# The operands of the second layer's first token block: formed during the first layer's last slots, four of them in a pool of their own

## The chip, the cores and the metric

The kernel runs on one core of one Trainium2 chip. The metric is the device time of one execution in microseconds (us), the median over several runs. TensorE (PE) does the matmuls and PEld is its weight load; VectorE is DVE, ScalarE is ACT, GpSimd is POOL, and SyncE (SP) issues every DMA.

## What is computed

A Nyström attention over 4 batches, 8 heads, 576 positions and 64 dimensions gives 2304 tokens of 512 values. Two feed-forward layers follow:

```python
a = x @ w_a; b = x @ w_b            # 512 -> 1536
x = (a * b) @ w_out                 # 1536 -> 512     the first layer
h = x @ w_in                        # 512 -> 2048     the second layer
sp = np.where(h > 20.0, h, np.log1p(np.exp(np.minimum(h, 20.0))))
out = (h * np.tanh(sp)) @ w_out2    # 2048 -> 512
```

## The kernel before, in words

**Number format.** Every operand of the large matmuls is stored as two float32r parts, a rounded "hi" and a remainder "lo". `split` (L327) makes them: ACT copies the source into hi, then another engine (DVE here, POOL for the products of the first layer) subtracts hi from the source into lo. One product takes three matmuls per 128 rows: hi·hi, hi·lo, lo·hi.

**First layer.** It runs as 96 slots (the loop at L621). Each slot makes one 128-row piece of a and of b (`emit_ab`, 12 matmuls), multiplies them on DVE (tile tg), splits the result (tile g1; hi on ACT, lo on POOL) and takes one entry off the queue `o1q` (`emit_o1`, 12 matmuls that multiply four older g1 tiles by the output weights, added up in `x2acc`). After the last slot four entries are left, and L661 to L663 emit them; all four read the g1 tiles of slots 92 to 95. Finished x2acc tiles are stored to DRAM (x2d) by L468. Beside slots 57 to 88 the weights of the second layer are converted and stored (`u2`, `to_dram`).

**Second layer.** It takes the tokens in three blocks of 768 (index pr) and the 2048 columns in eight chunks, which makes 24 steps n (the loop at L790). A block is four quadrants of x, "11", "12", "21", "22", each 384 tokens by 256 values. The product with a chunk of `w_in` is Winograd's form of Strassen's scheme, seven products instead of eight (`ORDER = 1, 6, 2, 7, 5, 4, 3`). The x operand of product k is a quadrant or a signed sum: t1 = 12 − 11, t2 = 22 − t1, t3 = 22 − 12, t4 = 21 − t2 (`X_OF`, L712). A product is 6 matmuls of 384 columns into one of two `ab` banks. What it gives is combined by DVE on eviction (u2s, c11, u3s, c22, u4s, c21, c12), passed through Mish on ACT and split again (g2). The weight operands are sums too (`weight_sums`, L499): `convert(n)` makes those of chunk n in the first block (four DVE sums, three splits) and stores them for the later blocks; `convert_o(n)` does the same for the output weights. After each product, the loop emits one or two of the twelve groups (`emit_o2`, 3 matmuls of 512 columns each) that multiply the previous step's g2 by the output weights; the list `GROUPS` gives their order.

**What is made early.** `x_early` (L541) is called in slots 90 to 95. It loads the four quadrants of block 0 into `stg` buffers, forms t1 and t2 in place, splits the operands of products 1, 6 and 2 into the pool `wp`, and makes the weight sums of chunk 0. After the last slot, `load_quads(0)` (L778) loads the same four quadrants a second time, and L781 to L789 form t3, t1, t2, t4 and split operands 7, 5, 4, 3 into the pool `p2`.

**Memory.** The pools share SBUF by place: `main` (weights, bm, wab, attention factors, x2acc) and above it `p1` (ta, tg and nine g1 buffers) stand on the left; `wp` stands on the right. After the last `emit_o1`, `p1` and `main` are closed and `p2` takes their place from the left. Its tiles lie in the order in which the code first asks for them: the quadrants, the sums, the operands 7, 5, 4, 3, then m1, u2s, the two wc, s4, c11, m, g2, u3s, wo and the rest. `reuse_waits="tile"` means that a tile waits only for those older tiles whose bytes it covers.

**Order of the work.** From L592 on, no engine's order is written out: a planner simulates the program and puts every engine's instructions in the order in which they become ready there, the earlier line of the program first where several are ready. On the chip each engine, and SP's DMA queue too, then goes through its own list strictly in order.

Of the kernel before, what the change touches and what calls it, by code (L numbers as in the profile page):

```python
# [8 lines left out]
F32 = mybir.dt.float32  # L9
F32R = mybir.dt.float32r  # L10
AF = mybir.ActivationFunctionType
ALU = mybir.AluOpType
# [19 lines left out]
def nystrom_moe_kernel(ctx: ExitStack, tc: tile.TileContext, q, k, v, w_a, w_b, w_out1, w_in2, w_out2, out):  # L32
    nc = tc.nc
    NT = B * S
    ve, gp = nc.vector, nc.gpsimd
# [25 lines left out]
    main = main_ctx.enter_context(tc.tile_pool(name="main", bufs=1, side="left"))  # L61
# [265 lines left out]
    def split(dst_hi, dst_lo, src, hi_eng, lo_eng, pin=False):  # L327
        if hi_eng is ac:
            i = ac.activation(dst_hi, src, AF.Copy)
            if pin:  # L330
                tc.keep_in_program_order(i)
        else:
            hi_eng.tensor_copy(out=dst_hi, in_=src)
        lo_eng.tensor_tensor(dst_lo, src, dst_hi.bitcast(F32), op=ALU.subtract)  # L334
# [20 lines left out]
    wab = {}  # L355
# [91 lines left out]
    def emit_o1(b, gp_, hf, d, part):  # L447

        if part == 0:
            o1p[0] = bank("o1")  # L450
        p = o1p[0]
        g = 2 * gp_ + part
        for ch in range(2):
            w, x = wo1[2 * g + ch], g1[b, g, hf, ch]
            for n, (sl, sr) in enumerate(((0, 0), (0, 1), (1, 0))):
                first, last = (part, ch, n) == (0, 0, 0), (part, ch, n) == (1, 1, 2)
                pe.matmul(p[:, 0:288], w[:, sl, 128 * d:128 * d + 128], x[:, sr, :], start=first, stop=last)
        if part == 0:
            return
        if gp_ == 0 and d == 0:  # L460
            x2acc[b, hf] = main.tile([128, 4, 288], F32, tag="x2", bufs=4, name="x2acc")
        dst = x2acc[b, hf][:, d]
        if gp_ == 0:
            ac.activation(dst, p[:, 0:288], AF.Copy)
        else:
            ve.tensor_tensor(dst, p[:, 0:288], dst, op=ALU.add)
        if gp_ == 2 and d == 3:
            nc.sync.dma_start(out=x2d[b][:, :, 288 * hf:288 * hf + 288], in_=x2acc[b, hf])  # L468
# [24 lines left out]
    TB = 384  # L493
# [5 lines left out]
    def weight_sums(dst, src, t):  # L499
        a11, a12, a21, a22 = src[:, 0:2, 0:128], src[:, 2:4, 0:128], src[:, 0:2, 128:256], src[:, 2:4, 128:256]  # L500
        ve.tensor_tensor(t[:, 0], a21, a22, op=ALU.add)
        ve.tensor_tensor(t[:, 1], t[:, 0], a11, op=ALU.subtract)
        ve.tensor_tensor(t[:, 2], a11, a21, op=ALU.subtract)
        ve.tensor_tensor(t[:, 3], a12, t[:, 1], op=ALU.subtract)
        split(dst[:, 0, 0:2], dst[:, 1, 0:2], src[:, :, 0:128].rearrange("p (a j) f -> p a j f", a=2), ac, ve)
        split(dst[:, 0, 2], dst[:, 1, 2], a22, ac, ve)
        split(dst[:, 0, 3:7], dst[:, 1, 3:7], t, ac, ve)

    def load_quad(t, i, half):

        off = 0
        while off < TB:
            b, s0 = divmod(i * TB + off, S)
            n = min(TB - off, S - s0)
            nc.sync.dma_start(out=t[:, :, off:off + n], in_=x2d[b][:, 2 * half:2 * half + 2, s0:s0 + n])
            off += n
# [1 line left out]
    xs = {}  # L518

    def x_tile(pr, k):  # L520
        pool, tag, bufs = (wp, "xe", 3) if k in (1, 6, 2) else (p2, "xc", 5)
        t = xs[pr, k] = pool.tile([128, 2, 2, TB], F32R, tag=tag, bufs=bufs, name="xc")
        return t

    def split_x(pr, k, src):
        t = x_tile(pr, k)
        split(t[:, 0], t[:, 1], src, ac, ve)
# [3 lines left out]
    def wc_tile(k):  # L531
        pool, tag, bufs = (wp, "we", 1) if k % 3 == 0 else (p2, "wc", 2)
        t = wc[k] = pool.tile([128, 2, 7, 2, 128], F32R, tag=tag, bufs=bufs, name="wc")
        return t

    def stg(shape, nm):
        return base.tile(shape, F32, tag="stg", bufs=3, name=nm)

    early = {}

    def x_early(n):  # L541

        if n == 0:
            for q, (i, half) in (("11", (0, 0)), ("12", (1, 0)), ("22", (1, 1))):
                early[q] = stg([128, 2, TB], "x" + q)
                load_quad(early[q], i, half)
        elif n == 1:
            split_x(0, 1, early["11"])
        elif n == 2:
            ve.tensor_tensor(early["12"], early["12"], early["11"], op=ALU.subtract)  # L550
            ve.tensor_tensor(early["22"], early["22"], early["12"], op=ALU.subtract)
            early["21"] = stg([128, 2, TB], "x21")
            load_quad(early["21"], 0, 1)
        elif n == 3:
            split_x(0, 6, early["22"])
            early["w"] = stg([128, 4, 256], "s_in")
            nc.sync.dma_start(out=early["w"], in_=wi2d[0])
        elif n == 4:
            split_x(0, 2, early["21"])
        elif n == 5:  # L560
            t = wc_tile(0)
            weight_sums(t, early["w"], stg([128, 4, 2, 128], "s4"))
            nc.sync.dma_start(out=wcd[0], in_=t.bitcast(F32).rearrange("p a k j f -> p (a k j f)"))
# [57 lines left out]
    for si, (b, w, hf, gi, ch) in enumerate(slots):  # L621
        ci, ks = divmod(si, 8)
        if si == 56:
            ap_ctx.close()
            wp = ctx.enter_context(tc.tile_pool(name="wp", bufs=1, side="right", reuse_waits="tile"))
# [4 lines left out]
        if si >= 90:  # L630
            x_early(si - 90)
# [29 lines left out]
    for u in o1q:  # L661
        emit_o1(*u, 0)
        emit_o1(*u, 1)  # L663
    p1_ctx.close()
    main_ctx.close()
    p2 = ctx.enter_context(tc.tile_pool(name="p2", bufs=1, side="left", reuse_waits="tile"))

# [8 lines left out]
    def fetch(k):  # L676

        if k < 8:
            f32s["i", k] = stg([128, 4, 256], "s_in")
            nc.sync.dma_start(out=f32s["i", k], in_=wi2d[k])  # L680
        elif k < 24:
            nc.sync.dma_start(out=wc_tile(k).bitcast(F32).rearrange("p a k j f -> p (a k j f)"), in_=wcd[k % 8])
# [18 lines left out]
    quads = {}  # L701

    def load_quads(pr):
        for q, (i, half) in (("11", (0, 0)), ("12", (1, 0)), ("22", (1, 1)), ("21", (0, 1))):
            quads[q] = p2.tile([128, 2, TB], F32, tag="xq", bufs=4, name="xq" + q)
            load_quad(quads[q], 2 * pr + i, half)

    def diff(nm, a, b):
        quads[nm] = p2.tile([128, 2, TB], F32, tag="tt", bufs=3, name="x" + nm)
        ve.tensor_tensor(quads[nm], quads[a], quads[b], op=ALU.subtract)  # L710

    X_OF = {1: "11", 6: "t2", 2: "21", 7: "t3", 5: "t1", 4: "t4", 3: "22"}  # L712

    def prepare(pr, k):
        if k == 1:
# [3 lines left out]
        if k == 4:  # L719
            diff("t4", "21", "t2")  # L720
        split_x(pr, k, quads[X_OF[k]])

# [19 lines left out]
    def ev(nm):  # L742
        return p2.tile([128, TB], F32, tag=nm, bufs=1, name=nm)
# [29 lines left out]
            t0 = (2 * pr + i) * TB + 128 * j  # L773
            nc.sync.dma_start(out=out[t0:t0 + 128], in_=o)

    GROUPS = [(c, i, j) for c, i in ((0, 0), (1, 1), (1, 0), (0, 1)) for j in range(3)]
    AT_GAP = (2, 2, 2, 2, 2, 1, 1)
    load_quads(0)  # L778
    fetch(1)
    fetch_o(0)  # L780
    for k in (7, 5, 4, 3):  # L781
        if k == 7:
            diff("t3", "22", "12")
        if k == 5:
            diff("t1", "12", "11")
            diff("t2", "22", "t1")
        if k == 4:
            diff("t4", "21", "t2")
        split_x(0, k, quads[X_OF[k]])  # L789
    for n in range(24):  # L790
        pr, nn = divmod(n, 8)
        o2 = [(n - 1, *g) for g in GROUPS] if n else []
        fetch(n + 2)
        fetch_o(n + 1)
        if nn == 5 and pr < 2:
            load_quads(pr + 1)
        for gap, k in enumerate(ORDER):
            p = product(k, n)
            if k == 1:
                m1 = ev("m1")  # L800
                ac.activation(m1, p[:, 0:TB], AF.Copy)
            elif k == 6:
                u2s = plus(p, m1, "u2s")
            elif k == 2:
                mish(2 * n, 0, plus(p, m1, "c11"))
            elif k == 7:
                u3s = plus(p, u2s, "u3s")
            elif k == 5:
                mish(2 * n + 1, 1, plus(p, u3s, "c22"))
                u4s = plus(p, u2s, "u4s")  # L810
            elif k == 4:
                mish(2 * n + 1, 0, plus(p, u3s, "c21"))
            else:
                mish(2 * n, 1, plus(p, u4s, "c12"))
            if nn == 7 and pr < 2:
                prepare(pr + 1, k)
            if gap == 1 and n + 1 < 8:
                convert(n + 1)
            if gap == 3 and n < 8:
                convert_o(n)  # L820
            for _ in range(AT_GAP[gap]):
                if o2:
                    emit_o2(*o2.pop(0))
    for g in GROUPS:
        emit_o2(23, *g)
# [36 lines left out]
```

## Time and profile before

| | us |
|---|---|
| median of 3 runs | 879.24 (876.66 to 885.28) |
| the profiled execution | 880.11 |
| its span on the core | 878.3 |
| PE busy | 808.9 (92%) |
| PEld busy | 698.0 (79%) |
| DVE busy | 552.1 (63%) |
| ACT busy | 346.3 (39%) |
| POOL busy | 102.4 (12%) |

The page of the profile cuts the span into 40 slices of 22 us, each digit a busy share in tenths. Two of its lines show the place that the change touches, in slices 22 and 23 (483 to 527 us); PEclk is the granted TensorE clock:

```profile
PE   4766899999999978999999599999999999999997
PEclk9678699999999979999999799999999999999999
```

Slots 90 to 95 lie at about 455 to 474 us of the span, the last `emit_o1` ends at about 481.4 us, and the second layer fills the rest. A wait in the trace is idle time of an engine, put down to the event that ended it; the idle time of an engine that is not the bottleneck costs nothing.

### The profile page before, as it was taken

How to read it: one execution, taken by the hardware profiler on the slowest of the kernel's cores; microseconds unless marked ns; L12 is line 12 of the kernel's file. 1: busy time of each engine (PE TensorE's matmuls, PEld its weight loads, DVE VectorE, ACT ScalarE, POOL GpSimd, SP SyncE). 2: the span in 40 equal slices, each digit the busy share in tenths (PEclk: the TensorE clock that was granted, in tenths of full speed). 3: DMA queues.
4: the chain of work that ended last, by engine and by line, in shares of the span. 5: the costliest groups of instructions: out<-in, count | busy, mean ns of one | idle time of the engine just before them, and what ended most of it. 6: DMA issues, size and time to landing. Idle time of an engine off the chain costs nothing.

```text
span 878.3 us, 14628 instructions
## 1 busy us (share of the span) xinstructions
PE 808.9 (92%) x5830; PEld 698.0 (79%) x5830; DVE 552.1 (63%) x1047; ACT 346.3 (39%) x689; POOL 102.4 (12%) x123
## 2 busy tenths in 40 slices
PE   4766899999999978999999599999999999999997
PEld 3445578887898947878998399888998898998985
DVE  7687868797366347789875996646634345443433
ACT  4234445435333434444433554435423234332322
POOL 0012211222141212212221000000000000000000
PEclk9678699999999979999999799999999999999999
DMA  9533656648433225877666997745755555654501
GB/s 356 226 115 109 240 156 227 233 150 304 172 136 128 85 91 165 290 241 232 199 220 215 385 411 290 263 180 216 261 181 197 193 180 215 233 181 186 180 1 72
DMA packets 48661, 178.25 MB, mean 203 GB/s; under 512 B 4176, under 2 KB 13904, under 8 KB 39504
## 3 DMA queue, kind: packets, MB, share of 16 engines
q1 hardware_dynamic: 48592, 177.31, 56.9%
q8 instruction: 46, 0.75, 0.3%
q14 instruction: 23, 0.19, 0.1%
HBM read 123.81 MB, written 53.48 MB: 202 GB/s over the span
## 4 chain that ended last, share of the span: by engine, by line
PE 70%; DVE 15%; DMA 6%; issue 4%; ACT 3%; POOL 1%; SPq 0%; ACTq 0%; DVEq 0%
PE ps_ab L49 31%; PE ps_o L49 19%; PE ps_bm L49 11%; PE ps_at L49 9%; DMA wi2d<-f 3%; DVE f L325 2%; DVE f L324 1%; DVE tg L437 1%; DVE f L323 1%; DVE f L320 1%; DMA wo2d<-f 1%; ACT f L317 1%; DMA qt<-in_q_dram 1%; ACT bm L49 1%; DVE xc L334 1%
## 5 line engine op out<-in xcount | busy, mean ns | idle before, releaser
L49 PE MATMUL ps_ab<-xc,wc 128*128 128x384 f32 x1008 | 195.4, 339 | 2.8 <-DVE xc L334 1.2
L49 PE MATMUL ps_ab<-at,bm 128*128 128x288 f32 x1152 | 187.3, 304 | 7.6 <-ACT ta L49 2.5
L49 PEld LDWEIGHTS ps_ab<-at,bm 128*128 128x128 f32 x1152 | 162.3, 191 | 38.4 <-issue 8.7
L49 PE MATMUL ps_o<-g,wo 128*128 128x288 f32 x1152 | 181.7, 300 | 10.3 <-ACT wo L49 4.3
L49 PEld LDWEIGHTS ps_ab<-xc,wc 128*128 128x128 f32 x1008 | 179.7, 188 | 13.0 <-ACT xc L49 2.6
L49 PEld LDWEIGHTS ps_o<-g,wo 128*128 128x128 f32 x1152 | 162.1, 190 | 24.2 <-issue 5.7
L49 ACT ACTIVATE m<-c 128x384 f32<-128x384 f32 x96 | 50.3, 524 | 186.7 <-DVE c L747 186.6
L334 POOL TENSOR_TENSOR g<-tg,g 128x288 fp32r<-128x288 f32 x96 | 85.2, 888 | 301.9 <-ACT g L49 301.9
L49 PE MATMUL ps_bm<-wo,g 128*128 128x512 f32 x288 | 94.0, 394 | 1.2 <-ACT osb L49 1.2
L49 PE MATMUL ps_at<-wo,g 128*128 128x512 f32 x288 | 82.5, 397 | 8.4 <-ACT g L49 8.4
L49 PE MATMUL ps_o<-wo,g 128*128 128x512 f32 x288 | 79.1, 395 | 0.0
L334 DVE TENSOR_TENSOR g<-m,g 128x384 fp32r<-128x384 f32 x96 | 53.5, 557 | 40.4 <-ACT g L49 37.7
L49 ACT ACTIVATE g<-tg 128x288 fp32r<-128x288 f32 x96 | 42.4, 442 | 71.8 <-DVE tg L437 71.0
L49 PEld LDWEIGHTS ps_at<-wo,g 128*128 128x128 f32 x288 | 53.8, 189 | 17.8 <-ACT g L49 8.8
L49 PEld LDWEIGHTS ps_bm<-wo,g 128*128 128x128 f32 x288 | 54.3, 189 | 13.0 <-ACT osb L49 1.6
L437 DVE TENSOR_TENSOR tg<-ps_ab,ta 128x288 f32<-128x288 f32 x96 | 43.3, 451 | 33.5 <-PE ps_ab L49 22.2
L49 ACT ACTIVATE ta<-ps_ab 128x288 f32<-128x288 f32 x96 | 39.0, 406 | 61.8 <-PE ps_ab L49 61.2
L49 PEld LDWEIGHTS ps_o<-wo,g 128*128 128x128 f32 x288 | 54.2, 190 | 9.4
L49 ACT ACTIVATE g<-m 128x384 fp32r<-128x384 f32 x96 | 50.3, 524 | 2.6
L747 DVE TENSOR_TENSOR u2s<-ps_ab,m 128x384 f32<-128x384 f32 x24 | 13.3, 556 | 46.8 <-PE ps_ab L49 46.8
L317 ACT ACTIVATE f<-stg 128x512 f32<-128x512 f32 x44 | 29.4, 671 | 33.8 <-DMA wi2d<-f 26.1
L334 DVE TENSOR_TENSOR bm<-ps_bm,bm 128x1024 fp32r<-128x1024 f32 x24 | 29.3, 1220 | 20.6 <-ACT bm L49 20.5
(142 smaller groups left out, 781.9 us busy)
## 6 DMA issues: line engine op xcount, KB each, us to landing
wc<-wcd SPq DMA_DIRECT2D x16, 1792.0 KB, 7.2
wo<-wod SPq DMA_DIRECT2D x16, 1024.0 KB, 4.8
stg<-in_moe_w_out_dram SPq DMA_DIRECT2D x28, 512.0 KB, 3.9
wcd<-wc SPq DMA_DIRECT2D x8, 1792.0 KB, 9.1
stg<-in_moe_w_in_dram SPq DMA_DIRECT2D x16, 512.0 KB, 4.8
wod<-wo SPq DMA_DIRECT2D x8, 1024.0 KB, 6.5
stg<-in_moe_w_a_dram SPq DMA_DIRECT2D x12, 512.0 KB, 5.3
stg<-in_moe_w_b_dram SPq DMA_DIRECT2D x12, 512.0 KB, 5.8
```

The lines of the kernel that those rows point to most:

```text
L49: i = f(*a, **kw)
L317: i = ac.engine.activation(dst, hi.bitcast(F32), AF.Abs)
L320: i = ve.tensor_scalar(dst, dst, F32_TINY, F32_HUGE, op0=ALU.max, op1=ALU.min)
L323: ve.tensor_scalar(du, du, 3, 0x3FFFFFFF, op0=ALU.logical_shift_left, op1=ALU.bitwise_and)
L324: ve.scalar_tensor_tensor(du, hi, 0xC0000000, du, op0=ALU.bitwise_and, op1=ALU.bitwise_or)
L325: ve.scalar_tensor_tensor(du, lo, 29, du, op0=ALU.logical_shift_right, op1=ALU.bitwise_or)
L334: lo_eng.tensor_tensor(dst_lo, src, dst_hi.bitcast(F32), op=ALU.subtract)
L437: ve.tensor_tensor(tg, pb[:, 0:288], ta, op=ALU.mult)
L747: ve.tensor_tensor(t, p[:, 0:TB], other, op=ALU.add)
```

## The change

`x_early` now loads all four quadrants at once in slot 90, into two tiles of the tag `wab` (three buffers of `main`, used until then for the first layer's weights), and takes a third one for t1 and t3; t2 and t4 overwrite "11" and "12". All four sums are formed there, in slots 91 to 94. After the last `emit_o1`, with `p1` closed but `main` still open, a new pool `px` of four buffers opens on the right, and operands 7, 5, 4, 3 are split into it. `load_quads(0)` and the loop that made these operands in `p2` are gone; `p2` no longer holds five operand buffers, and blocks 1 and 2 use the four of `px`. Two orders change as well. `GROUPS` goes through j as 2, 0, 1 for i = 0 (unchanged for i = 1). `convert(n + 1)` moves from the gap after the second product to the gap after the fifth (after the fourth in step 0), and `convert_o(0)` to the gap after the sixth.

```diff
     def x_tile(pr, k):
-        pool, tag, bufs = (wp, "xe", 3) if k in (1, 6, 2) else (p2, "xc", 5)
+        pool, tag, bufs = (wp, "xe", 3) if k in (1, 6, 2) else (px, "xc", 4)
...
+    X_OF = {1: "11", 6: "t2", 2: "21", 7: "t3", 5: "t1", 4: "t4", 3: "22"}
     early = {}
 
     def x_early(n):
 
         if n == 0:
-            for q, (i, half) in (("11", (0, 0)), ("12", (1, 0)), ("22", (1, 1))):
-                early[q] = stg([128, 2, TB], "x" + q)
-                load_quad(early[q], i, half)
-        elif n == 1:
-            split_x(0, 1, early["11"])
-        elif n == 2:
-            ve.tensor_tensor(early["12"], early["12"], early["11"], op=ALU.subtract)
-            ve.tensor_tensor(early["22"], early["22"], early["12"], op=ALU.subtract)
-            early["21"] = stg([128, 2, TB], "x21")
-            load_quad(early["21"], 0, 1)
-        elif n == 3:
-            split_x(0, 6, early["22"])
+            for (q0, f0), (q1, f1) in ((("11", (0, 0)), ("12", (1, 0))), (("22", (1, 1)), ("21", (0, 1)))):
+                t = main.tile([128, 2, 2, TB], F32, tag="wab", bufs=3, name="xq")
+                for h, (q, f) in enumerate(((q0, f0), (q1, f1))):
+                    early[q] = t[:, h]
+                    load_quad(t[:, h], *f)
             early["w"] = stg([128, 4, 256], "s_in")
             nc.sync.dma_start(out=early["w"], in_=wi2d[0])
+        elif n == 1:
+            t = main.tile([128, 2, 2, TB], F32, tag="wab", bufs=3, name="xt")
+            early["t1"], early["t3"] = t[:, 0], t[:, 1]
+            split_x(0, 1, early["11"])
+            ve.tensor_tensor(early["t1"], early["12"], early["11"], op=ALU.subtract)
+        elif n == 2:
+            early["t2"] = early["11"]
+            ve.tensor_tensor(early["t2"], early["22"], early["t1"], op=ALU.subtract)
+            split_x(0, 6, early["t2"])
+        elif n == 3:
+            split_x(0, 2, early["21"])
+            ve.tensor_tensor(early["t3"], early["22"], early["12"], op=ALU.subtract)
         elif n == 4:
-            split_x(0, 2, early["21"])
+            early["t4"] = early["12"]
+            ve.tensor_tensor(early["t4"], early["21"], early["t2"], op=ALU.subtract)
...
     p1_ctx.close()
+    px = ctx.enter_context(tc.tile_pool(name="px", bufs=1, side="right", reuse_waits="tile"))
+    for k in (7, 5, 4, 3):
+        split_x(0, k, early[X_OF[k]])
     main_ctx.close()
...
-    GROUPS = [(c, i, j) for c, i in ((0, 0), (1, 1), (1, 0), (0, 1)) for j in range(3)]
+    GROUPS = [(c, i, (j - 1 + i) % 3) for c, i in ((0, 0), (1, 1), (1, 0), (0, 1)) for j in range(3)]
     AT_GAP = (2, 2, 2, 2, 2, 1, 1)
-    load_quads(0)
     fetch(1)
     fetch_o(0)
-    for k in (7, 5, 4, 3):
-        if k == 7:
-            diff("t3", "22", "12")
-        if k == 5:
-            diff("t1", "12", "11")
-            diff("t2", "22", "t1")
-        if k == 4:
-            diff("t4", "21", "t2")
-        split_x(0, k, quads[X_OF[k]])
...
-            if gap == 1 and n + 1 < 8:
+            if gap == 4 - (n == 0) and n + 1 < 8:
                 convert(n + 1)
-            if gap == 3 and n < 8:
+            if gap == 3 + 2 * (n == 0) and n < 8:
                 convert_o(n)
```

## Rows read from the trace of the kernel before

**Rows 1.** Busy time by stretch: from:to length, PE PEld DVE ACT POOL, PEclk, DMA share, GB/s

```profile
446.40:474.00 27.60, 26.16 (x188) 24.99 (x188) 19.68 (x35) 11.57 (x24) 6.78 (x8) 1.00 0.71 234
474.00:482.50 8.50, 8.22 (x55) 7.66 (x53) 2.75 (x7) 1.76 (x4) 0.81 (x1) 1.00 0.67 239
482.50:490.90 8.40, 0.01 (x1) 0.00 (x0) 6.32 (x12) 5.16 (x7) 0.00 (x0) 0.79 0.96 310
490.90:498.80 7.90, 6.72 (x21) 4.22 (x21) 7.90 (x13) 2.93 (x4) 0.00 (x0) 0.79 1.03 432
498.80:506.60 7.80, 6.22 (x21) 5.24 (x22) 7.19 (x12) 5.00 (x8) 0.00 (x0) 0.78 1.01 394
```

**Rows 2.** Timeline, 482 to 507 us: start, length, engine, line, operation [idle before, releaser]

```profile
482.59 3.74 SPq L515 DMA_DIRECT2D xq<-x2d  x6
...
485.67 1.06 ACT L49 ACTIVATE wo<-s_out 128x1024 fp32r<-128x1024 f32 x1 [9.25 <-DMA x2d<-x2acc]
...
490.94 1.22 PE L49 MATMUL ps_at<-wo,g 128*128 128x512 f32 x2 [8.44 <-ACT g L49]
...
506.63 2.28 PE L49 MATMUL ps_ab<-xc,wc 128*128 128x384 f32 x12
```

**Rows 3.** PE's matmuls from 482.52 to 506.62 us by shape: count, busy us, mean ns

```profile
L49 PE MATMUL ps_ab<-xc,wc 128*128 128x384 f32 x24 | 7.0, 405 | 2.7 <-DVE xc L334 1.2 <-DVE u4s L747 0.7 <-ACT xc L49 0.6
L49 PE MATMUL ps_at<-wo,g 128*128 128x512 f32 x6 | 3.0, 600 | 8.4 <-ACT g L49 8.4
L49 PE MATMUL ps_bm<-wo,g 128*128 128x512 f32 x6 | 2.5, 473 | 0.0
L49 PE MATMUL ps_o<-wo,g 128*128 128x512 f32 x6 | 2.4, 530 | 0.0
```

**Rows 4.** Chain that ended last, undisturbed stretch: start, length, work

```profile
559.80 0.69 PE ps_o L49 x3
...
561.18 2.10 PE ps_ab L49 x12
```

**Rows 5.** DVE, then ACT, from 482.52 to 506.62 us by shape

```profile
L334 DVE TENSOR_TENSOR wo<-s_out,wo 128x1024 fp32r<-128x1024 f32 x3 | 3.7, 1222 | 2.1 <-ACT wo L49 2.1
L334 DVE TENSOR_TENSOR xc<-xt,xc 128x768 fp32r<-128x768 f32 x3 | 2.8, 950 | 0.0
...
L334 DVE TENSOR_TENSOR wc<-s,wc 128x1024 fp32r<-128x1024 f32 x2 | 2.4, 1216 | 0.0
...
L503 DVE TENSOR_TENSOR s<-s_in 128x256 f32<-128x256 f32 x3 | 1.2, 416 | 0.0
...
L334 DVE TENSOR_TENSOR g<-m,g 128x384 fp32r<-128x384 f32 x2 | 1.1, 550 | 0.0
...
L747 DVE TENSOR_TENSOR u2s<-ps_ab,m 128x384 f32<-128x384 f32 x1 | 0.5, 549 | 0.0
...
L49 ACT ACTIVATE xc<-xt 128x768 fp32r<-128x768 f32 x3 | 2.4, 833 | 3.6 <-DVE xt L710 3.6
```

**Rows 6.** Timeline around 453 us: a DVE and a POOL instruction together

```profile
453.23 0.82 POOL L334 TENSOR_TENSOR g<-tg,g 128x288 fp32r<-128x288 f32 x1 [1.76 <-ACT g L49]
453.31 1.56 DVE L334 TENSOR_TENSOR xc<-x,xc 128x768 fp32r<-128x768 f32 x1
```

**Rows 7.** Waits from 446 to 482 us

```profile
DVE x L551 <- DMA x<-x2d: 2.3, 1, 2.3
...
PE ps_o L49 <- POOL g L334: 0.2, 1, 0.2
```

**Rows 8.** Waits from 866 us to the end

```profile
ACT osb L49 <- DMA out_dram<-osb: 1.6, 1, 1.6
...
PE ps_bm L49 <- ACT osb L49: 1.2, 1, 1.2
```

**Rows 9.** Timeline, 522 to 524 us

```profile
522.69 0.47 ACT L49 ACTIVATE m<-ps_ab 128x384 f32<-128x384 f32 x1
...
523.75 0.67 SPq L694 DMA_DIRECT2D wcd<-wc  x1
```

More of the change, by code (lines that the diff above doesn't have):

```diff
@@ L710, in diff @@
         ve.tensor_tensor(quads[nm], quads[a], quads[b], op=ALU.subtract)
-    X_OF = {1: "11", 6: "t2", 2: "21", 7: "t3", 5: "t1", 4: "t4", 3: "22"}
     def prepare(pr, k):
```

## The prediction, made before the run

> **What bounds the kernel now.** I first read the busy shares by slice, then the busy time by stretch around the change of layers. PE is busy all but 1.4 of 27.6 us in the last slots and 8.22 of the next 8.50 us; then comes 0.01 of 8.40 us, and two stretches at a granted clock of 0.79 and 0.78 in which DVE is the full engine (7.90 of 7.90, 7.19 of 7.80) [rows 1]. So PE bounds the kernel except from 482.5 us, where product 2 of step 0 ends, to 506.6 us, where step 1 begins.
>
> Next the timeline there. PE's 8.44 us end with an ACT result: the Mish of product 2. ACT could not make it, because in its list `convert_o(0)` stood ahead and waited 9.25 us for the store of the last x2acc, whose bytes tile wo covers. Meanwhile block 0's quadrants, which cover weights that the last `emit_o1` reads, are loaded again from 482.59 us [rows 2]. Then DVE forms t3, t1, t2, t4 and the lo parts of operands 7, 5, 4, 3, all in front of PE.
>
> What this costs: in the 24.1 us PE does 24 product matmuls and 18 output matmuls [rows 3]. Undisturbed, 12 product matmuls take 2.10 us and three output matmuls 0.69 [rows 4]: 24 × 0.175 + 18 × 0.23 = 8.3 us. **15.8 us are lost**: 9.2 of them because the matmuls' busy time adds up to only 14.9 us, and 6.6 because those 14.9 us are not 8.3.
>
> **The change, part by part.**
>
> *Sums and operands 7 and 5 beside the slots.* Sums t3 and t4 and, if their buffers are free, two lo parts come on top of DVE's list there: 4 × 0.95 = 3.8 us at the lo row's duration (same columns, two inputs), and 2 × 0.83 on ACT [rows 5]. DVE is idle for 7.9 us before 474.0 us and for 5.75 after [rows 1]; this covers it. Without that cover, tg comes late and PE with it, by up to 3.8 us. The six quadrant loads were issued in these slots before too; now they go out together in slot 90. SP's list delays nothing more by them than before: stores of converted weights and the load of chunk 0's weights stand behind. DVE's wait of 2.3 us for a quadrant [rows 7] should shrink, since all come at once. I charge 0.5 us; bounds 0 and 3.8.
>
> Here a row speaks against the change: one DVE lo part next to a POOL lo part took 1.56 us, not 0.95 [rows 5, 6]. PE has waited just 0.2 us for POOL in these slots [rows 7], so the rows charge nothing beyond the 0.5. Four more collisions of 0.6 us on the path would make it 2.4. The Trainium skill ("GPSIMD Engine Reference", section "Key points") says that POOL shares its SBUF interfaces with DVE, with contention when a DVE instruction has two SBUF inputs. By that rule all four added instructions may collide, and the sum below would be 1.9 us worse; the long row agrees with it.
>
> *Which buffers are free.* By the sizes in the code, px (four times 6 KB) lies over p1's g1 buffers (nine times 2.25 KB). The last four entries read four neighbouring ones; the two px buffers in the middle cover those, the two outer ones don't. So I expect two operands done by about 477 us and two only after the last `emit_o1`, about 481.5 us: 0.83 on ACT, then twice 0.95 on DVE.
>
> *ACT's 9.25 us go.* With xq, sums and operands (51 KB) no longer first in p2, wo falls onto wab and attention factors, and no tile of step 0 onto x2acc; wc falls onto bm and weights that are free at 474 us. What is late next is DVE.
>
> *Gone from the stall:* the second quadrant load with SP's 3.74 us of issue [rows 2], four sums (3.8 us of DVE), two of four operands.
>
> *What remains after 481.5 us.* On DVE: two lo parts 1.9; seven evictions at 0.55, 3.85; four g2 lo parts at 0.55, 2.2; weight conversion for step 1: four sums at 0.42, a lo part of 1.22 and two of 768 columns together, an estimate of 1.1 from the 0.95 row, 4.0; wo 1.22 [rows 5]. Sum 13.2 us, so DVE ends at 494.7 us; with conversion, wo and one eviction moved into DVE's 5.75 idle us (5.8 us of work), at 488.9. PE needs until 482.5 + 8.3 = 490.8 for the same work. DVE therefore holds PE by between 0 and 3.9 us; the chain from the last `emit_o1` to operand 4 (0.83 + 0.95) and Mish's table load add up to 2 more. I take **3.3 us lost instead of 15.8: a gain of 12.5**; ends 15.8 and, if ACT gets stuck on another older buffer as before, 3.
>
> *Later conversion.* `convert` now stands behind the fifth product. Its cover is that the planner moves it ahead: at 523.75 us the fifth store since slot 95 goes out, chunk 4's, while step 2's first eviction starts at 522.69 [rows 9], so conversion runs nearly two steps ahead of use and its place in the code hardly binds. Cost 0; without the cover see rival 3.
>
> *Four operand buffers instead of five* remove the spare at the two block changes: an operand is split only after the product that reads the old one, seven products before its own use. Cost 0; bound 1 us each.
>
> *GROUPS.* At the end, PE waits 1.2 us for an ACT eviction of the same bank pair and ACT 1.6 us for an output buffer [rows 8]. j = 2 first puts that eviction two groups (1.4 us) earlier: gain 1.0, bounds 0 and 1.2. At the two block changes j = 2 now needs the bank pair evicted last, but a product (1.05 us) lies between. Cost 0, bound 1 each.
>
> *Sum.* 12.5 + 1.0 − 0.5 = 13.0 us. The profiled execution took 880.11 us, 1.8 of it around the span: 867.1. The median of the runs is 0.9 lower, and its runs spread more than that; I predict **867.0 us**.
>
> **The rivals.**
>
> *1. The stall moves to DVE or ACT and half stays.* The planner may put other ready work, such as block 1's quadrants and sums, into the freed time: DVE was full from 490.9 us on [rows 1], which speaks for it. Against it: 9.25 us of the stall were one wait that has no cause any more. Price: 4 us idle and 4 from slow matmuls, as the 6.6 us above came on top of 9.2 idle. Gain 15.8 − 8 + 1.0 − 0.5 = 8.3: 871.8 us. On the clock the rows show 1.00 before the stall, and 0.79 and 0.78 in the stretches after it [rows 1]. The Trainium skill ("TensorE: Matmul & The Clock Gate", section "What's actually happening") calls the slow state the default that activity releases. By that rule any idle stretch left over is paid twice, which the rows bear out.
>
> *2. The change doesn't do what it says.* All four px operands wait for the end of `emit_o1`, conversions of step 1 wait for the sums' buffers (s4 lies over a wab buffer that t4 is made in), and a wait at the head of ACT's or DVE's list holds the rest. Then 12 of the 15.8 us stay: 879 less 3.8 and what the end gives or the slots take, 874 to 880. For it: the order comes from a simulation, and it put that ACT wait there in the first place.
>
> *3. Slower: conversion where the code has it.* Place: steps 1 to 6. After the fifth product a step has two products (2.1 us) and four groups (2.8 us) left, 4.9 us of PE. Conversion needs 4.0 us of DVE, with two evictions and three g2 lo parts (2.75 us) between, and before its last lo part an ACT copy of 1024 columns, 1.1 us by the 0.83 row [rows 5]: 7.85. If the planner leaves it there, each step loses 3 us, 18 in all; less 13.0 that is +5, with the two bounds at the block changes +9: 884 to 889 us. It decides as soon as the last lo part of a chunk comes later than its step's second product. Against it: the two steps of lead [rows 9].
>
> **How the numbers follow.** Forecast 0.62 (its own range 862.5 to 870.4), rival 1 0.18 (870 to 875), rival 2 0.12, rival 3 0.08. The low end, 862.5, is nothing lost in the stall and the median's offset; the high end, 876.5, takes in rival 1 and the near part of rival 2. Within 1% of 879.24 (8.8 us, about what a measurement of this kernel can tell from no change) lies what ends above 870.4: faster 0.62 + 0.04 (a fifth of rival 1) = 0.66; same 0.14 + 0.12 + 0.03 = 0.29; slower the rest of rival 3, 0.05.
>
> **What would show each step.** Right: in the timeline the splits of two px operands before the last `emit_o1` ends, no DMA releaser ahead of ACT's wo, no quadrant loads behind the last x2acc store except block 1's; PE busy in nearly all of the 10 us after 482.5 and step 1's first product near 490 us; clock 1.00 there; at the end no 1.2 us wait for the eviction. Wrong: a PE wait above 3 us on DVE operands (rival 1), on an older buffer (rival 2), or PE waits on weight splits wc in steps 2 to 7 (rival 3). PE idle of over 2 us in the slots would make the first charge too small.

## The result, and the profile after

| | before | after |
|---|---|---|
| median, us | 881.38 (875.52 to 885.28, 10 runs) | 873.56 (871.17 to 874.97, 10 runs) |
| ratio, 95% interval | | 0.9912 [0.9889, 0.9935] |
| the profiled execution, its span | 880.11, 878.3 | 874.2, 872.4 |
| PE, DVE, ACT, POOL busy | 808.9, 552.1, 346.3, 102.4 | 810.0, 549.9, 345.8, 104.9 |

The change gains 7.8 us (5.7 to 9.8 by the interval); 13.0 were forecast. The two lines of the page that cut the span into 40 slices show that the stall became shorter and did not go away: slice 22 has PE at 7 where it had 5, and the clock still at 7.

```profile
PE   4777799999999978999999799999999999999997
PEclk9568599999999979999999799999999999999999
```

The busy time by stretch, in the columns of [rows 1], says where:

```profile
446.40:474.00 27.60, 26.77 (x198) 26.28 (x197) 19.33 (x40) 9.79 (x23) 8.81 (x9) 1.00 0.77 271
474.00:482.50 8.50, 7.38 (x51) 6.92 (x49) 2.12 (x6) 2.65 (x4) 0.82 (x1) 1.00 0.15 53
482.50:490.90 8.40, 5.03 (x15) 4.01 (x16) 8.40 (x16) 6.61 (x11) 0.00 (x0) 0.61 0.94 287
490.90:498.80 7.90, 7.18 (x28) 6.15 (x27) 7.90 (x14) 2.90 (x6) 0.00 (x0) 0.77 1.01 411
498.80:506.60 7.80, 7.80 (x39) 6.94 (x39) 7.32 (x15) 5.58 (x11) 0.00 (x0) 1.00 1.01 387
```

In the slots PE is as busy as before. But the sums are not there: the planner puts the quadrant loads at 417 us and all four sums between 424.53 and 429.84 us, some 25 us ahead of slot 90. PE's one wait near them is for an x2acc eviction that stands on DVE behind two of the sums:

```profile
424.53 0.94 DVE L556 TENSOR_TENSOR xt<-xq 128x768 f32<-128x768 f32 x1
...
426.76 1.85 PE L49 MATMUL ps_o<-g,wo 128*128 128x288 f32 x12 [0.86 <-DVE x2acc L466]
```

From 482.5 to 490.9 us PE now works for 5.03 us instead of 0.01, but not for 8.4. The mean granted clock of 0.61 there and the 0.77 behind it say that part of the work ran at 1.2 GHz.

The timeline of the changed kernel there, ACT's lines first, then DVE's, then PE's (start, length, engine, line, operation, and in brackets the idle time before it with its releaser):

```profile
474.42 1.56 ACT L49 ACTIVATE xc<-xt 128x768 fp32r<-128x768 f32 x2
481.76 1.58 ACT L49 ACTIVATE xc<-xq 128x768 fp32r<-128x768 f32 x2 [5.78 <-PE ps_o L49]
483.25 0.47 ACT L49 ACTIVATE m<-ps_ab 128x384 f32<-128x384 f32 x1
...
484.45 1.05 ACT L49 ACTIVATE wo<-s_out 128x1024 fp32r<-128x1024 f32 x1
...
481.70 0.46 DVE L466 TENSOR_TENSOR x2acc<-ps_o,x2acc 128x288 f32<-128x288 f32 x1 [1.12 <-PE ps_o L49]
482.08 1.82 DVE L334 TENSOR_TENSOR xc<-xt,xc 128x768 fp32r<-128x768 f32 x2
483.81 1.82 DVE L334 TENSOR_TENSOR xc<-xq,xc 128x768 fp32r<-128x768 f32 x2
...
486.55 0.55 DVE L755 TENSOR_TENSOR u2s<-ps_ab,m 128x384 f32<-128x384 f32 x1
...
489.43 0.55 DVE L755 TENSOR_TENSOR c<-ps_ab,m 128x384 f32<-128x384 f32 x1
...
478.23 3.44 PE L49 MATMUL ps_o<-g,wo 128*128 128x288 f32 x24 [0.29 <-DVE x2acc L466]
483.77 1.87 PE L49 MATMUL ps_ab<-xc,wc 128*128 128x384 f32 x6 [2.10 <-ACT m L49]
487.16 2.29 PE L49 MATMUL ps_ab<-xc,wc 128*128 128x384 f32 x6 [1.52 <-DVE u2s L755]
490.03 2.29 PE L49 MATMUL ps_ab<-xc,wc 128*128 128x384 f32 x6 [0.58 <-DVE c L755]
...
497.25 1.31 PE L49 MATMUL ps_ab<-xc,wc 128*128 128x384 f32 x6 [0.71 <-DVE u4s L755]
...
499.79 1.22 PE L49 MATMUL ps_ab<-xc,wc 128*128 128x384 f32 x6
```

ACT's wo is free of the store (the 9.25 us of [rows 2] are gone). In their place ACT stands for 5.78 us before the hi parts of operands 4 and 3, which may be written only when the last `emit_o1` has read the g1 tiles under them. Behind them in ACT's list stands m1, the copy of product 1, which PE had finished before 475 us: it empties an `ab` bank, so PE cannot begin product 2 before 483.77. m1's own buffer does not hold it up: it lies over the fifth of the twelve chunks of the first layer's output weights, and the last entries read only the last four. On DVE the lo parts of operands 7 and 5, whose hi parts were done at 476, come behind the last x2acc eviction, and u2s behind all four lo parts and three weight sums.

From the end of the last `emit_o1` (478.23 + 3.44 = 481.67 us) to step 1's first product (499.79) there are 18.1 us, in which PE does 30 product and 15 output matmuls, 30 × 0.175 + 15 × 0.23 = 8.7 us by [rows 4]. **9.4 us are lost**: 4.9 in the four waits above (2.10 + 1.52 + 0.58 + 0.71), 4.5 in matmuls that run longer, most of them at the low clock; a product that takes 1.22 us at 499.79 took 2.29 at 487.16. In the kernel before the same count gives 15.8 of 25.2. So the stall gave 6.4 us, the last `emit_o1` ends 0.2 later, the steps between the stall and the end took some 0.2 longer, and the end gave nothing: from the last pair of products to the end of the span it is 14.9 us in both. The two spans differ by 5.9 us; the medians differ by more because the two profiled executions stand differently in their spreads.

The end of the changed kernel, PE's last line and ACT's last, which answer to [rows 8]:

```profile
865.11 0.84 PE L49 MATMUL ps_at<-wo,g 128*128 128x512 f32 x3
...
868.73 0.60 ACT L49 ACTIVATE osb<-ps_bm 128x512 f32<-128x512 f32 x1 [1.66 <-DMA out_dram<-osb]
```

PE's wait of 1.2 us has gone. ACT's for the output buffer has not, and the last eviction is behind it.

### The profile page after: what moved, and what is told of

It is laid out like the page before. It is cut to its first block, busy times and chain, and to the rows that moved or that the text cites. A ratio compares the mean times of both kernels' runs of the same rounds, so it can differ in the third digit from the quotient of the medians.

```text
span 872.4 us, 14607 instructions
## 1 busy us (share of the span) xinstructions
PE 810.0 (93%) x5830; PEld 700.6 (80%) x5830; DVE 549.9 (63%) x1045; ACT 345.8 (40%) x689; POOL 104.9 (12%) x123
## 4 chain that ended last, share of the span: by engine, by line
PE 71%; DVE 13%; DMA 8%; issue 3%; ACT 3%; SPq 1%; POOL 1%; ACTq 0%; DVEq 0%
PE ps_ab L49 31%; PE ps_o L49 19%; PE ps_bm L49 12%; PE ps_at L49 10%; DMA wi2d<-f 3%; DMA stg<-in_moe_w_a_dram 2%; DVE f L325 1%; DVE f L324 1%; DMA stg<-in_moe_w_out_dram 1%; DMA wo2d<-f 1%; DVE f L320 1%; ACT f L317 1%; DMA xq<-x2d 1%; DVE f L323 1%; DVE tg L437 1%
## 5 line engine op out<-in xcount | busy, mean ns | idle before, releaser
L49 PE MATMUL ps_ab<-xc,wc 128*128 128x384 f32 x1008 | 200.9, 342 | 5.0 <-ACT m L49 2.1
L49 PEld LDWEIGHTS ps_ab<-xc,wc 128*128 128x128 f32 x1008 | 182.2, 190 | 16.7 <-ACT m L49 2.3
L334 POOL TENSOR_TENSOR g<-tg,g 128x288 fp32r<-128x288 f32 x96 | 87.7, 915 | 297.0 <-ACT g L49 297.0
L755 DVE TENSOR_TENSOR c<-ps_ab,m 128x384 f32<-128x384 f32 x24 | 13.4, 557 | 52.3 <-PE ps_ab L49 52.3
```

The costliest lines, as they stand in the source:

```text
L49: i = f(*a, **kw)
L755: ve.tensor_tensor(t, p[:, 0:TB], other, op=ALU.add)
```

## The experiments

Each was timed beside the kernel before on one chip. "Lost" is counted as above, from the last `emit_o1` to step 1's first product, in the one profiled execution of each kernel, and so does not depend on when the first layer ends there. groups_old, osb_four and convert_old, which leave the waits of the stall as they are in the changed kernel, lose 9.4 us like it.

| kernel | median, us | before | ratio, 95% interval | lost, us |
|---|---|---|---|---|
| changed kernel | 873.56 | 881.38 | 0.9912 [0.9889, 0.9935] | 9.4 |
| m1_first | 869.92 | 882.34 | 0.9863 [0.9841, 0.9884] | 6.1 |
| lo_pool | 871.57 | 882.34 | 0.9892 [0.9868, 0.9915] | 10.0 |
| groups_old | 873.28 | 882.34 | 0.9901 [0.9881, 0.9920] | 9.4 |
| osb_four | 872.11 | 882.34 | 0.9876 [0.9853, 0.9899] | 9.4 |
| m1_c11 | 867.16 | 882.47 | 0.9833 [0.9799, 0.9867] | 3.7 |
| m1_lo_pool | 870.42 | 882.47 | 0.9866 [0.9833, 0.9899] | 7.5 |
| convert_old | 872.02 | 882.47 | 0.9892 [0.9860, 0.9925] | 9.4 |
| m1_c11_osb | 866.92 | 882.47 | 0.9825 [0.9792, 0.9859] | 3.1 |
| before_wo_late | 881.31 | 880.77 | 1.0013 [0.9991, 1.0035] | 14.4 |
| m1_c11_pool_osb | 865.90 | 880.77 | 0.9835 [0.9802, 0.9868] | 1.4 |
| before_wo_place | 881.35 | 882.08 | 0.9986 [0.9962, 1.0010] | 15.3 |

**m1_first.** Is the rest of the stall the order in the lists, or DVE's amount of work?

```diff
-    for k in (7, 5, 4, 3):
+    for k in (7, 5):
         split_x(0, k, early[X_OF[k]])
...
+    p = product(1, 0)
+    m1_0 = base.tile([128, 512], F32, tag="f24", bufs=2, name="m1")[:, 0:TB]
+    ac.activation(m1_0, p[:, 0:TB], AF.Copy)
+    p = product(6, 0)
+    u2s_0 = base.tile([128, 512], F32, tag="f24", bufs=2, name="u2s")[:, 0:TB]
+    ve.tensor_tensor(u2s_0, p[:, 0:TB], m1_0, op=ALU.add)
+    for k in (4, 3):
+        split_x(0, k, early[X_OF[k]])
```

> The kernel after, but products 1 and 6 of step 0 and their evictions (m1 on ACT, u2s on DVE, into f24 buffers) stand ahead of the splits of operands 4 and 3. Theory A (head of the list: m1 stood behind two copies that wait 5.8 us for the end of the first layer, and u2s behind it): product 2 starts at about 481.7 instead of 483.8 us and product 7 no longer waits for u2s; of the 9.4 us that PE still loses there 4 to 5 come back: 868.5 to 869.5 us. Theory B (DVE was the full engine from 482.5 to 498.8 us, whatever its order): the same DVE work has to be done before step 1, at most 1 us comes back: 872.5 to 873.5.

Lost falls from 9.4 to 6.1 us, 3.3 of the 4 to 5 that theory A said, and the time to 869.92, a little above A's interval and well below B's. DVE's lines, then PE's:

```profile
481.43 1.82 DVE L334 TENSOR_TENSOR xc<-xt,xc 128x768 fp32r<-128x768 f32 x2
483.17 1.82 DVE L334 TENSOR_TENSOR xc<-xq,xc 128x768 fp32r<-128x768 f32 x2
484.90 0.55 DVE L764 TENSOR_TENSOR c<-ps_ab,m 128x384 f32<-128x384 f32 x1
...
485.60 4.18 PE L49 MATMUL ps_ab<-xc,wc 128*128 128x384 f32 x12 [2.01 <-DVE c L764]
```

Product 2 is done before the last `emit_o1` ends, and the next instruction of the same kind is in the way: c11, which empties product 2's bank, behind four lo parts.

**lo_pool.** All four lo parts on POOL, the rest as in the changed kernel.

```diff
-        split_x(0, k, early[X_OF[k]])
+        t = x_tile(0, k)
+        split(t[:, 0], t[:, 1], early[X_OF[k]], ac, gp)
```

> The kernel after, but the lo parts of operands 7, 5, 4, 3 of block 0 are made by POOL (about 2.2 us each by its 0.81 us for 288 columns) instead of DVE; the order on ACT stays. Theory B (DVE-bound): 3.8 us of DVE work go from the stall, PE's 2.1 us wait for m1 stays: 3 to 4 us come back, 869.5 to 870.5. Theory A (head of ACT's list): m1 still comes at 483.3 and product 2 at 483.8, u2s only 1 to 2 us earlier: 871.5 to 873.5.

The time, 871.57 us, lies in theory A's interval and above B's. (The profiled execution is the slowest of the six, 876.52 us.) The window from 482.5 us, then PE's lines, then DVE's:

```profile
482.50:490.90 8.40, 4.11 (x18) 3.36 (x17) 5.03 (x9) 5.00 (x9) 3.59 (x2) 0.72 0.70 229
```

```profile
485.56 1.79 PE L49 MATMUL ps_ab<-xc,wc 128*128 128x384 f32 x6 [2.10 <-ACT m L49]
489.54 2.29 PE L49 MATMUL ps_ab<-xc,wc 128*128 128x384 f32 x6 [2.19 <-DVE u2s L756]
...
486.32 2.02 DVE L501 TENSOR_TENSOR s<-s_in 128x256 f32<-128x256 f32 x1 [2.37 <-POOL xc L334]
```

DVE is now idle for 3.4 of 8.4 us, and PE waits as before: 2.10 us for m1, which still stands behind the blocked hi parts in ACT's list, and 2.19 for u2s. The second wait has a new cause. u2s stands on DVE behind the weight sums; the first of these waits 2.37 us for POOL's lo part of operand 4, as its tile s4 lies over the tile that holds t4, and then takes 2.02 us beside POOL instead of 0.42. So work taken off the engine that looked full gave nothing here, but the run moves a wait as well as work, and by itself does not show what DVE's amount of work costs.

**groups_old** and **osb_four** ask what the end is worth: the old order of j, and four output buffers of their own instead of the two shared ones.

```diff
-    GROUPS = [(c, i, (j - 1 + i) % 3) for c, i in ((0, 0), (1, 1), (1, 0), (0, 1)) for j in range(3)]
+    GROUPS = [(c, i, j) for c, i in ((0, 0), (1, 1), (1, 0), (0, 1)) for j in range(3)]
```

> The kernel after with the order of GROUPS as before (j = 0, 1, 2). If the forecast's term holds, PE's 1.2 us wait at the end returns and costs 1.0: 874.6. Theory C (the end is set by the two output buffers, whose DMA the last eviction waits for in both traces): PE's wait returns, the time stays within 0.4 us: 873.2 to 874.0; the two block changes show no PE wait above 0.3 us in either order.

```diff
-            o = base.tile([128, DM], F32, tag="f24" if j else "stg", bufs=2 if j else 3, name="osb")
+            o = (p2 if j else base).tile([128, DM], F32, tag="osb" if j else "stg", bufs=4 if j else 3, name="osb")
```

> The kernel after with four output buffers of their own for j = 1 and 2 instead of the two f24 buffers. Theory C: the last eviction's wait of 1.66 us for an output DMA goes and the end comes 1.5 to 1.7 us earlier: 871.9 to 872.1. If the output DMAs themselves or SP's issue set the end, nothing comes back: 873.2 to 874.

The end of groups_old, PE and ACT, and then of osb_four, ACT:

```profile
865.39 0.97 PE L49 MATMUL ps_bm<-wo,g 128*128 128x512 f32 x3 [1.18 <-ACT osb L49]
...
867.01 0.60 ACT L49 ACTIVATE osb<-ps_o 128x512 f32<-128x512 f32 x1 [1.68 <-DMA out_dram<-osb]
```

```profile
865.99 0.59 ACT L49 ACTIVATE osb<-ps_o 128x512 f32<-128x512 f32 x1
866.47 0.60 ACT L49 ACTIVATE osb<-ps_bm 128x512 f32<-128x512 f32 x1
```

With the old order PE's wait is back, and from the last products to the end it is 14.94 us against 14.89: the new order is worth nothing. With four buffers ACT does not wait, and it is 13.79 us: 1.1 us come back, of the 1.5 to 1.7 that theory C said. The times agree with C, but their intervals overlap with the changed kernel's; it is the traces that show it. Two waits ran side by side, the forecast paid for the one that PE showed, and the one for the buffer ends last.

**m1_c11.** m1_first with product 2 and c11 moved ahead too; m1, u2s and c11 get buffers at the low end of px, over old tg tiles.

```diff
+    E = {nm: px.tile([128, TB], F32, tag=nm + "0", bufs=1, name=nm) for nm in ("m1", "u2s", "c11")}
...
+    p = product(2, 0)
+    ve.tensor_tensor(E["c11"], p[:, 0:TB], E["m1"], op=ALU.add)
     for k in (4, 3):
```

> The changed kernel, with step 0's products 1, 6 and 2 and their three evictions (m1, u2s, c11) issued ahead of the splits of operands 4 and 3; the three evictions go into buffers of their own in px, over the old tg tiles, which are free at 474 us, so that none waits for the end of the last emit_o1. In m1_first (869.92 us, step 1's first product at 494.79) c11 still lay over a live wo1 buffer and came behind four lo parts on DVE, at 484.9, and PE waited 2.0 us for it. Theory D (what is left of the stall is order and buffers: c11 holds Mish of c11, and PE): step 1's first product about 1.5 to 2.0 us earlier, near 493; 868.0 to 868.5 us. Rival E (DVE's amount of work holds PE from 482.5 us on, it was busy 8.40 of 8.40 there in m1_first): the eviction moved ahead is worth its own 0.55 us at most, 869.4 to 869.9 us.

867.16 us, somewhat better than theory D said, and lost falls to 3.7. (Step 1's first product comes at 491.81, also because the planner now puts most output matmuls behind it; the count of what is lost allows for that.) The interval of the ratio overlaps with m1_first's, so against rival E it is the trace that speaks. What is left is one wait, 1.69 us for u2s, which stands behind the lo parts of 7 and 5 on DVE, and slow matmuls behind it. m1_c11_osb, below, has the same order here and the same wait, but the clock did not fall. PE's line of m1_c11, then that of m1_c11_osb:

```profile
485.21 6.30 PE L49 MATMUL ps_ab<-xc,wc 128*128 128x384 f32 x24 [1.69 <-DVE u2s L690]
...
482.12 4.04 PE L49 MATMUL ps_ab<-xc,wc 128*128 128x384 f32 x18 [1.69 <-DVE u2s L690]
```

The granted clock is 0.80 from 482.5 to 490.9 us in the first and 1.00 from 474 us on in the second, which loses 3.1 us instead of 3.7.

**m1_lo_pool.** m1_first, with the lo parts of 4 and 3 on POOL.

> m1_first with the lo parts of operands 4 and 3 on POOL (those of 7 and 5 stay on DVE). Rival E (DVE's amount of work): 1.9 us less on DVE between 482.5 and 490.9 us, where it was full, and step 1 begins 1.5 us or more earlier: about 868.4 us. Theory D (order: c11 and Mish): c11 comes behind two lo parts instead of four, 1.9 us earlier as well, but operands 4 and 3 are ready at about 484.3 and 486.1 us (1.8 us each on POOL) instead of 484.4, and DVE's four sums are longer beside POOL (2.0 us for one against about 1.0 in the run with all four lo parts on POOL); the two cancel within 0.5 us: 869.4 to 870.4 us.

No gain over m1_first, and 1.4 us more lost. The time is at the upper end of theory D's interval and 2 us above rival E's. But DVE did not get free, as E supposes: it is busy 8.40 of 8.40 us from 482.5 us here too, so this run does not decide against E. DVE's lines and POOL's (the first line takes in the second):

```profile
480.38 3.45 DVE L334 TENSOR_TENSOR xc<-xt,xc 128x768 fp32r<-128x768 f32 x2
481.25 2.58 DVE L334 TENSOR_TENSOR xc<-xt,xc 128x768 fp32r<-128x768 f32 x1
483.76 0.55 DVE L765 TENSOR_TENSOR c<-ps_ab,m 128x384 f32<-128x384 f32 x1
...
480.99 4.54 POOL L334 TENSOR_TENSOR xc<-xq,xc 128x768 fp32r<-128x768 f32 x2 [8.33 <-ACT xc L49]
```

Two DVE lo parts take 3.45 us here and 1.82 in the changed kernel.

**convert_old.** Conversion at its old places in the code.

```diff
-            if gap == 4 - (n == 0) and n + 1 < 8:
+            if gap == 1 and n + 1 < 8:
                 convert(n + 1)
-            if gap == 3 + 2 * (n == 0) and n < 8:
+            if gap == 3 and n < 8:
```

> The changed kernel, with convert(n + 1) and convert_o(n) put back to the gaps of the kernel before (after the second and fourth product). The forecast (place in the code hardly binds, the planner runs conversion two steps ahead): 0 in steps 1 to 7; in step 0 the sums and split of chunk 1's weights may come ahead of c11 on DVE, at most 2 us: 873.6 to 875 us. Rival 3 turned round (the later place costs 3 us in each of six steps): the old place would be faster by up to 18 us, under 870 us.

872.02 us, ratio 0.9892 against 0.9912 with overlapping intervals, and 9.4 us lost in both: the place in the code is worth nothing that these runs can tell.

**before_wo_late** and **before_wo_place** ask the opposite question: in the kernel before, was ACT's wait of 9.25 us the stall? The first moves `convert_o(0)` in the code:

```diff
-            if gap == 3 and n < 8:
+            if gap == 3 + 2 * (n == 0) and n < 8:
```

> The kernel before, with one line changed: convert_o(0) stands in the gap after the sixth product of step 0, as in the changed kernel, so that ACT comes to wo later; sums, quadrants and operands stay as before. Theory F (ACT's 9.25 us wait was the stall, the early sums hardly matter): Mish of c11 no longer stands behind it, and most of the 7.8 us come back, 874 to 876 us. Rival G (behind that wait the sums and operands on DVE are next, as the forecast said: in the trace of before DVE idles only 2.7 of the 24.1 us between product 2 of step 0 and step 1): at most 2.7 us, 879 to 881 us beside a before of about 882.

It did not do what it was made for. ACT's wait is still there: the planner left wo where it was.

```profile
487.93 1.06 ACT L49 ACTIVATE wo<-s_out 128x1024 fp32r<-128x1024 f32 x1 [9.39 <-DMA x2d<-x2acc]
```

So the second asks for wo's tile ahead of m1, and the wait goes:

```diff
-        t, f = wo_tile(k), f32s.pop(("o", k))
+        t, f = wo2[0] if k == 0 else wo_tile(k), f32s.pop(("o", k))
...
+    wo_tile(0)
     for n in range(24):
```

> The kernel before, with the tile wo of step 0 asked for ahead of m1, so that it lies over bm and wab tiles that are free at 474 us; only the first g2 tile now covers the last x2acc. (before_wo_late kept ACT's wait, 9.39 us: the planner left wo where it was in ACT's list, so it could not tell F from G.) Theory F (ACT's wait for the store was the stall): 874 to 876 us beside a before of about 881. Rival G (behind it, the quadrants, which land at about 490 us, and DVE's sums and lo parts set step 1): PE starts the output matmuls about 2 us earlier, at 488.5 to 489 instead of 490.9, and step 1's first product comes 0 to 2.7 us earlier: 878.5 to 881 us.

ACT's line, then DVE's, then PE's, of before_wo_place:

```profile
477.99 1.05 ACT L49 ACTIVATE wo<-s_out 128x1024 fp32r<-128x1024 f32 x1
...
488.00 0.55 DVE L747 TENSOR_TENSOR c<-ps_ab,m 128x384 f32<-128x384 f32 x1
...
491.87 1.82 DVE L710 TENSOR_TENSOR xt<-xq,xq 128x768 f32<-128x768 f32 x2 [1.85 <-DMA xq<-x2d]
...
489.71 1.22 PE L49 MATMUL ps_at<-wo,g 128*128 128x512 f32 x2 [5.54 <-ACT g L49]
490.74 1.05 PE L49 MATMUL ps_bm<-wo,g 128*128 128x512 f32 x2
494.22 1.22 PE L49 MATMUL ps_at<-wo,g 128*128 128x512 f32 x2 [2.43 <-DVE g L334]
```

The longest wait of the stall is taken away, PE's first wait falls from 8.44 to 5.54 us, and the time stays: 0.9986 [0.9962, 1.0010], with 15.3 us lost instead of 15.8 (before_wo_late, where the wait is still there, loses 14.4, so 0.5 us is no gain). What ends PE's first wait is now c11, late in DVE's list, and PE pays the rest a little later, while DVE waits for the quadrants. Theory F falls, and rival G holds at its low end. That the change gained by the rest, no second load and sums ahead of time, follows by elimination; no run takes out one of these alone.

**m1_c11_osb** and **m1_c11_pool_osb** put the pieces together: m1_c11 with four output buffers, and then with the lo parts of operands 7 and 5 on POOL, which is idle there.

> m1_c11 together with the four own output buffers of osb_four. The two places lie 370 us apart and share no buffer, so the gains add: m1_c11's time less the 1.1 us that the end took less in osb_four. Theory D: 866.9 to 867.4 us; rival E: 868.3 to 868.8 us.

> m1_c11 with four own output buffers, and the lo parts of operands 7 and 5 on POOL, which is idle from about 477 us on (with all four lo parts on POOL it made these two by 480.8 us, 1.8 us each, beside the x2acc evictions). In m1_c11 DVE makes them only after the last x2acc eviction, u2s stands behind them and PE waits 1.69 us for it. Theory D (order on DVE's list): that wait goes and c11 follows, 1.5 to 1.8 us less than m1_c11_osb (866.92 us): 865.1 to 865.5 us. Rival H (DVE is full anyway from 482.5 us on and operands 4 and 3 then hold PE instead; or POOL beside DVE stretches the x2acc evictions, on which the last emit_o1 hangs): 866.5 to 868 us.

m1_c11_osb came out at 866.92, in D's interval but only 0.2 under m1_c11, whose runs spread over 3 us. The times alone do not show the 1.1; the trace does, with 13.75 us from the last pair of products to the end. The last one gave 865.90, a little above what D expected and below H. Its windows, POOL's line and PE's:

```profile
474.00:482.50 8.50, 8.21 (x57) 7.98 (x57) 1.86 (x5) 2.42 (x5) 4.41 (x3) 1.00 0.21 75
482.50:490.90 8.40, 7.92 (x40) 6.31 (x39) 8.40 (x17) 7.36 (x13) 0.00 (x0) 1.00 0.78 258
490.90:498.80 7.90, 7.48 (x35) 5.85 (x34) 7.90 (x13) 4.02 (x7) 0.00 (x0) 1.00 0.95 327
```

```profile
476.03 3.65 POOL L334 TENSOR_TENSOR xc<-xt,xc 128x768 fp32r<-128x768 f32 x2
...
482.18 5.26 PE L49 MATMUL ps_ab<-xc,wc 128*128 128x384 f32 x24
```

From the last `emit_o1` on PE does four products without a wait, the clock stays at 1.00 (2.4 GHz), and 1.4 us are lost of the 15.8 with which the study began. DVE is as full as in the changed kernel, 8.40 of 8.40 us, so a full DVE does not by itself hold PE there. To the kernel before the ratio is 0.9835 [0.9802, 0.9868], clear of the changed kernel's; from m1_c11 and m1_c11_osb the times do not tell it apart, and the last step (3.1 to 1.4 us lost) rests on the traces.

## Why the prediction was right, and where it was not

The time is inside the range and on the forecast's side, but the forecast's 13.0 us lie outside the measured 5.7 to 9.8, and 873.56 lies outside the forecast's own part of the range (up to 870.4). The gain is 0.9%, just short of the 1% that I gave 0.66. By its size this is rival 1, that half of the stall stays (871.8 us); the mechanism that kept it is close to the one of rival 2, a wait at the head of ACT's and DVE's lists, though two operands waited for the last `emit_o1` and not all four. The sign that I set for both rivals, one PE wait above 3 us, did not come: there are four shorter ones, the longest 2.10 us. Nor did two of the signs of being right: step 1's first product came at 499.79 and not near 490, and the clock was 0.61.

- **The stall, 12.5 forecast, 6.4 measured.** This is the mis-sized term. The step that failed is "DVE therefore holds PE by between 0 and 3.9 us": I added up DVE's work and compared it with PE's, as if DVE could do it in the order in which PE needs it. m1_first and m1_c11 show that the order bound: with the same work, moving evictions ahead took the 9.4 us lost to 6.1 and 3.7 (3.1 in m1_c11_osb), and two lo parts on POOL took it to 1.4. The sum was short too: DVE works without a gap from 482.08 us to step 1, 17.7 us against the 13.2 added up, as all four lo parts, a second wo and three sums of block 1 lie there and none of the 5.8 us of work moved ahead. But in m1_c11_pool_osb DVE is as full, and PE hardly waits. And the chain that I let "add up to 2 more" is 3.1 us: 0.83 + 0.95, and 1.28 for the table load in both traces.
- **Which buffers are free.** Right: two operands have their hi parts by 476 us, the other two wait for the last `emit_o1` (5.78 us on ACT). Wrong is "two operands done by about 477": the lo parts waited on DVE until 482.08. And I did not ask what stands behind the two blocked ones in ACT's list, as my own bound of 3 us ("if ACT gets stuck on another older buffer as before") would have had me do.
- **ACT's 9.25 us.** They went, as forecast. But I counted them as the greater part of the 15.8, and before_wo_place shows that alone they are worth nothing that could be measured: DVE's list and the quadrants were right behind.
- **The clock.** The rule that I weighed, that any idle time left over is paid twice, holds in the changed kernel: 4.9 us of waits come with 4.5 us in slower matmuls, and in m1_c11_pool_osb, where the waits are gone, the clock is 1.00. It does not hold for every wait: after the same 1.69 us the clock fell in m1_c11 (0.80) and not in m1_c11_osb (1.00). The Trainium skill ("TensorE: Matmul & The Clock Gate", section "What's actually happening") has the slow state as the default; the rows after the longer stalls agree.
- **The end, 1.0 forecast, 0.0 measured.** The mechanism was half right: PE's wait went, but I did not follow ACT's 1.6 us, which I had named in the same sentence, to the last eviction.
- **The slots, 0.5 forecast.** The work did not come beside slots 90 to 95: the planner formed the sums at 424 to 430 us, where PE has one wait of 0.86 us. In the slots PE is busy 26.77 of 27.6 us, and the last `emit_o1` ends 0.2 us later; in the profiled executions of the three kernels with m1_c11's order it ended between 479.4 and 482.5 us, so the term is too small to see.
- **Later conversion and four buffers, 0 forecast.** Right: convert_old, and no PE wait on a weight split or at the block changes in the trace after.
- **The price of rival 3** (conversion left where the code has it, 884 to 889 us) had no place to act: the planner moves it.

## What to carry to other kernels

An engine that goes through its list in order is not a sum of work but a queue: when an instruction is put early, ask what it can wait for, and what that somebody needs now stands behind it. Here the two hi parts that were asked for early blocked a copy of 0.47 us on which TensorE hung, and putting three short evictions ahead of the blocked splits (m1_c11) gave about as much again as the change. The longest wait in a stall is not its price: take it away alone before you credit it, as the next one may stand right behind; and give an early tile a place over something that is really finished.

## What the hardware showed that was not expected

POOL makes a lo part of 128x768 in 1.82 us (3.65 for two), against DVE's 0.95. When both do it at once, as in m1_lo_pool, the rows read as if one waited for the other. DVE's first lo part, begun before POOL's, took its 0.95 us; the second took 2.58, from 481.25 to 483.83, while POOL's first ran to 483.02. POOL's two took 2.03 and 2.55 us, and a DVE sum of 128x256 that began beside the second took 1.12 us instead of 0.42. A DVE eviction beside it, which reads one operand from PSUM, kept its 0.55 us (c11 at 483.76). The Trainium skill ("GPSIMD Engine Reference", section "Key points") says that the two share SBUF interfaces, with contention when a DVE instruction has two SBUF inputs, and that DVE is about twice as fast at elementwise work; the rows agree with both. In the prediction the collision was put at 0.6 us an instruction; here one lo part on DVE lost nothing and the other 1.6. In these runs the lo parts helped on POOL only where DVE made evictions meanwhile (m1_c11_pool_osb), not where it had lo parts or sums of its own (m1_lo_pool, lo_pool).
